# Two attention blocks with a gate on one core: score matmuls issued twice at accumulator closings, first loads on one queue, last output tiles summed in freed banks

## Chip, cores and metric

One core of one Trainium2 chip. The metric is device time in microseconds (us) of one execution; lower is better. The kernel before took 888.87 us at first (median of 3 runs, 887.62 to 891.12).

Engine names: PE is TensorE (matmul), PEld its weight loads, ACT is ScalarE, DVE is VectorE, POOL is GpSimd, SP is SyncE, which only issues transfers. "Granted clock" is the share of full speed that the throttle lets TensorE run at; the trace shows only 1.00 and 0.50.

## The reference, cut

```python
# x: (1, 2048, 512) bf16; 32 heads of 16
def _A_ref(x, wqkv, wo):                 # full attention
    q, k, v = split(x @ wqkv)
    p = softmax(einsum("bhqd,bhkd->bhqk", q, k) * 16 ** -0.5)
    return merge(einsum("bhqk,bhkd->bhqd", p, v)) @ wo

def _B_ref(x, wqkv, wo):                 # each query sees 8 keys, 2 apart
    ...
g = sigmoid((x * gate_w).sum(-1, keepdims=True))
return g * _A_ref(x, A_wqkv, A_wo) + (1 - g) * _B_ref(x, B_wqkv, B_wo)
```

Attention A costs 32 x 2048 x 2048 exponentials. ACT computes most of them, and DVE the rest with a polynomial.

## The kernel before

The program is written out by a planner (`Plan`) that simulates the engines with assumed durations and decides in which order each engine's instructions are emitted. Every change of an assumed duration can therefore reshuffle the order of all engines.

The main loop fills a PSUM ring of 3 or 2 banks with score matmuls, and ACT takes the exponential of the whole ring bank group in one instruction:

```python
def f():                                             # one fill of the ring, on PE
    for s_, (p_, t, j) in enumerate(units):
        qk_mm(ring[:, s_, :], p_, t, j)              # start=True: overwrites its bank
    ...                                              # (cut: one more unit for DVE)
yield ("pe", 0, dur, f)
...
def f():                                             # then, on ACT
    A.activation(out=st["pT"][:, 0:n, :], in_=ring[:, 0:n, :], func=ACT.Exp, ...)
```

The products with V are accumulated in one bank, `acc`, over a period (four heads, 512 queries); 32 periods follow each other. At the end of a period `acc` is closed: DVE copies it out, and until then PE can add nothing to it. So that PE looks busy to the clock's throttle, gaps are filled with dummy matmuls that add zero to the open `acc` or write an idle bank:

```python
HAM = 3.4133
share = 0.70
def idle_fill(self, st, room):
    ...
    have = sum(b - max(a, lo) for a, b in self.streamed)   # streaming in the last 3.41 us
    need = min(gap, self.share * self.HAM - have)
    ...                                                    # fill `need` with dummies
```

The loads of the first microseconds, and the times at which the planner assumes that they have landed:

```python
A.dma_start(out=wkr[:], in_=a_w3[:, :, D:2 * D])           # all of K's weights, ACT's queue
for sc in range(NC):                                       # four chunks of x, SP's queue
    SP.dma_start(out=xr[sc // 2][:, sc % 2], in_=...)
A.dma_start(out=wqr[:], in_=a_w3[:, :, 0:D])
...
XARR = (6.0, 8.0, 10.0, 12.0)
```

K's first projections are evicted by DVE (`kt_all`), which then takes their maximum (`kmax_all`). The last query chunk's output is computed in two pieces because one of its inputs comes very late: 7 of 8 products go to an SBUF tile `fpart`, and after the last period one product is added:

```python
def part():
    V.tensor_copy(out=fpart["t"][:, tt, :], in_=w.t[:])
...
yield ("pe", tt, MM + SW, tail, "w")                       # the eighth product
yield from out_steps(t, w, fpart["t"][:, tt, :], tt)       # DVE adds, SP stores
```

## Time and profile before

| kernel before | |
|---|---|
| span of the profiled run | 886.6 us |
| ACT busy | 839.2 us, 95% |
| first exponential starts | 20.84 us |
| stream of 726 exponentials, first start to last end | 854.31 us |
| last exponential's end to the end of the span | 11.50 us |
| mean granted clock | 0.978 |

From the page of the kernel before: the span; busy time with its share of the span and the number of instructions; the granted clock in 40 slices, in tenths; and two groups of instructions with "busy, mean ns | idle before, releaser".

```profile
span 886.6 us, 15806 instructions
...
PE 768.4 (87%) x5958; PEld 270.6 (31%) x6020; DVE 772.5 (87%) x1354; ACT 839.2 (95%) x751; POOL 619.2 (70%) x594
...
PEclk9799999999999999999999999999997999999999
...
L283 ACT ACTIVATE pT<-ring 128x1536 bf16<-128x1536 f32 x726 | 831.0, 1301 | 26.6 <-PE ring L283 16.8
L283 PE MATMUL ring<-qt,kt_all 32*128 32x512 bf16 x1814 | 288.2, 387 | 88.0 <-ACT pT L283 76.6
```

ACT is the engine that bounds the stream, and its idle time is mostly waiting for the ring to be filled (16.8 us). Where these waits lie is seen in stretches of 10 us (columns: stretch, its length, busy time of each engine with the count of instructions, granted clock, DMA share, GB/s); kernel before:

```profile
30.00:40.00 10.00, 9.78 (x74) 2.71 (x72) 5.72 (x12) 8.57 (x8) 0.00 (x0) 0.60 0.00 1
...
660.00:670.00 10.00, 7.92 (x53) 2.70 (x51) 8.66 (x17) 8.34 (x7) 9.69 (x11) 0.81 0.43 145
670.00:680.00 10.00, 9.55 (x56) 2.52 (x57) 7.02 (x12) 7.38 (x7) 9.84 (x9) 0.68 0.00 0
...
400.00:410.00 10.00, 9.02 (x67) 3.04 (x68) 8.29 (x17) 9.88 (x10) 5.10 (x8) 1.00 0.08 27
```

Where the clock is full, ACT is busy 9.88 of 10 us; where it is granted 0.60 to 0.81, only 7.4 to 8.6. In this profile the clock is low from 27.8 (for 10.24 us), 287.2 (3.41), 372.6 (6.83), 427.2 (3.41), 666.1 (10.24) and 799.2 us (3.41), and in a last stretch that the end of the kernel cuts. The complete ones are all multiples of 3.41 us, as the Trainium skill has it ("TensorE: Matmul & The Clock Gate", Part 1): two clock levels, decided in free-running windows of 3413 ns by how busy PE was.

The chain of waits of the kernel before in the first 24 us (start us, length us, what):

```profile
1.77 9.22 DMA xr<-in_A_x_dram
11.00 0.05 issue
11.04 1.08 PE xt L283 x16
...
15.97 0.69 DVE kmax_all L283
...
17.25 0.67 DVE kt_all L283
...
17.95 0.70 DVE kmax_all L283
...
20.84 3.71 ACT pT L283 x3
```

The chain to the first exponential begins with a load: x's third chunk lands at 11.0 us, and only then its 16 transposes (`xt`) start. Over the profile the four chunks' transposes start at 6.29, 8.94, 11.04 and 12.81 us.

The end of the kernel before, from its timeline (start us, length us, engine, line, operation, [idle before <- releaser]):

```profile
875.20 1.96 PE L283 MATMUL w<-ident,z 128*32 128x512 bf16 x9
875.61 0.69 DVE L283 COPY accS<-acc 128x512 f32<-128x512 f32 x1 [3.58 <-PE acc L283]
877.09 0.66 PE L283 MATMUL w<-identf,accS 128*128 128x128 f32 x4
...
880.10 1.29 DVE L283 TENSOR_TENSOR osb<-w,fpart 128x512 bf16<-128x512 f32 x2 [0.48 <-PE w L283]
...
882.62 1.30 DVE L283 TENSOR_TENSOR osb<-w,fpart 128x512 bf16<-128x512 f32 x2 [1.22 <-DMA out_dram<-osb]
```

Nine dummies delay the transposes of the last accumulator by 0.8 us, and the third output waits 1.22 us for a store to free its buffer.

### The profile page before, as it was taken

What the parts mean: (1) busy time and instruction counts of PE and PEld (TensorE: products, weight loads), DVE (VectorE), ACT (ScalarE), POOL (GpSimd) and SP (SyncE); (2) the same over time, 40 slices, a digit from 0 to 9 for tenths busy, and PEclk for the clock granted to TensorE, in tenths of its full rate; (3) what the DMA queues carried; (4) which work ended last, traced back from release to release, by engine and by line L of the source; (5) the groups of instructions that cost most, each with busy time, mean ns of one, the idle gap of its engine ahead of it and who ended that gap; (6) DMA issues with size and microseconds to landing.
All of it is one profiled execution on the core that took longest, in us unless ns stands there. A gap on an engine that the chain in (4) does not pass through costs nothing.

```text
span 886.6 us, 15806 instructions
## 1 busy us (share of the span) xinstructions
PE 768.4 (87%) x5958; PEld 270.6 (31%) x6020; DVE 772.5 (87%) x1354; ACT 839.2 (95%) x751; POOL 619.2 (70%) x594
## 2 busy tenths in 40 slices
PE   7998889998898888889889998888889988878886
PEld 4332333333223233222223233323322223222222
DVE  5689889988989899989888889999997989998885
ACT  3999999999999999989999999999998999999994
POOL 2000283899797899897898989898999798964000
PEclk9799999999999999999999999999997999999999
DMA  8002213330414230320030403113021230100000
GB/s 286 2 1 95 65 39 115 111 120 28 147 35 143 75 105 24 109 80 28 8 119 31 131 28 115 55 54 108 1 89 43 78 120 14 58 8 1 1 1 25
DMA packets 54653, 59.78 MB, mean 67 GB/s; under 512 B 2592, under 2 KB 51232, under 8 KB 54576
## 3 DMA queue, kind: packets, MB, share of 16 engines
q1 hardware_dynamic: 52992, 57.71, 20.4%
q10 hardware_dynamic: 1584, 1.05, 0.4%
q8 instruction: 47, 0.77, 0.4%
q14 instruction: 30, 0.25, 0.1%
HBM read 46.14 MB, written 12.62 MB: 66 GB/s over the span
## 4 chain that ended last, share of the span: by engine, by line
ACT 44%; PE 21%; issue 18%; DVE 15%; DMA 1%; POOL 0%; SPq 0%; another core or an unknown queue 0%; ACTq 0%; DVEq 0%
ACT pT L283 44%; PE w L283 9%; DVE ta L283 8%; PE ring L283 7%; PE acc L283 6%; DVE pd L283 2%; DMA xr<-in_A_x_dram 1%; DVE lg L283 1%; DVE accS L283 1%; DVE kt_all L283 0%; ACT lg L283 0%; DVE ssum L283 0%; DVE kvs L283 0%; DVE kmax_all L283 0%; DVE kpk L283 0%
## 5 line engine op out<-in xcount | busy, mean ns | idle before, releaser
L283 ACT ACTIVATE pT<-ring 128x1536 bf16<-128x1536 f32 x726 | 831.0, 1301 | 26.6 <-PE ring L283 16.8
L283 PE MATMUL ring<-qt,kt_all 32*128 32x512 bf16 x1814 | 288.2, 387 | 88.0 <-ACT pT L283 76.6
L283 DVE SCALAR_TENSOR_TENSOR ta<-ta,w 128x512 f32<-128x512 f32 x468 | 309.9, 681 | 5.1
L283 POOL TENSOR_TENSOR prod<-prod 128x512 f32<-128x512 f32 (+1 forms) x208 | 241.3, 1172 | 6.0
L283 PE MATMUL acc<-pT,vp_all 128*17 128x512 bf16 x1814 | 232.8, 391 | 0.1
L283 PEld LDWEIGHTS <-kt_all 32*128 32x128 bf16 x2048 | 105.0, 91 | 336.3 <-issue 320.4
L283 DVE TENSOR_SCALAR ta<-w 128x512 f32<-128x512 uint16 x234 | 158.4, 685 | 43.5 <-PE w L283 42.0
L283 PE MATMUL acc<-ident,z 128*32 128x512 bf16 (+4 forms) x756 | 170.3, 339 | 9.1 <-DVE accS L283 9.0
L283 DVE SCALAR_TENSOR_TENSOR pd<-ta,w 128x512 uint16<-128x512 f32 x234 | 157.1, 679 | 2.5
L283 POOL TENSOR_TENSOR prod<-ksh,qb 128x512 f32<-128x512 bf16 x128 | 145.7, 1166 | 11.4 <-DMA ksh<-kv_scr 9.2
L283 POOL TENSOR_TENSOR prod<-vsh,lg 128x512 f32<-128x512 bf16 x128 | 136.5, 1099 | 10.6 <-DVE lg L283 8.3
L283 PE MATMUL w<-qt,kt_all 32*128 32x512 bf16 x234 | 88.5, 388 | 1.3 <-DVE pd L283 1.2
L283 POOL TENSOR_SCALAR mq<-qpk 128x512 f32<-128x512 bf16 x12 | 7.5, 628 | 106.9 <-DVE qpk L283 106.9
L283 PE MATMUL acc<-pd,vp_all 128*17 128x512 bf16 x234 | 81.0, 391 | 0.0
L283 PEld LDWEIGHTS <-z 128*32 128x32 bf16 x796 | 54.2, 95 | 84.6 <-issue 65.6
L283 PEld LDWEIGHTS <-vp_all 128*17 128x17 bf16 x2048 | 43.9, 88 | 90.4 <-issue 88.8
L283 PE MATMUL w<-bw,xT 128*128 128x512 bf16 x160 | 49.1, 394 | 5.8 <-DVE pd L283 2.8
L283 PEld LDWEIGHTS <-xT 128*128 128x128 bf16 x512 | 31.8, 98 | 38.1 <-issue 26.1
L283 POOL TENSOR_TENSOR lg<-lg,mx 128x256 f32<-128x256 f32 x16 | 10.1, 631 | 44.6 <-DVE mx L283 44.6
L283 DVE CAST kvs<-w 128x512 bf16<-128x512 f32 x32 | 22.0, 687 | 12.1 <-PE w L283 11.9
L283 DVE COPY accS<-acc 128x512 f32<-128x512 f32 x32 | 21.8, 682 | 3.6 <-PE acc L283 3.6
L283 PE MATMUL w<-identf,accS 128*128 128x128 f32 x128 | 21.9, 296 | 0.1
(97 smaller groups left out, 439.2 us busy)
## 6 DMA issues: line engine op xcount, KB each, us to landing
ksh<-kv_scr SPq DMA_DIRECT2D x16, 1024.0 KB
vsh<-kv_scr SPq DMA_DIRECT2D x16, 1024.0 KB
kv_scr<-kvs SPq DMA_DIRECT2D x16, 256.0 KB
kt_all<-k_scr SPq DMA_DIRECT2D x6, 512.0 KB
q_scr<-qpk SPq DMA_DIRECT2D x24, 128.0 KB
qt<-q_scr SPq DMA_DIRECT2D x24, 128.0 KB
xr<-in_A_x_dram SPq DMA_DIRECT2D x4, 512.0 KB
out_dram<-osb SPq DMA_DIRECT2D x16, 128.0 KB
```

Source lines behind the costliest of these rows:

```text
L283: return chain_on(self._key, f(*a, **k))
```

## The change

Four intents:

1. *Closings.* While `acc` is closed and the planner's estimate of streaming in the last window is under 0.60, the ring's score matmuls are issued twice. They overwrite, so the result is the same and PE is busier. This adds 64 matmuls.
2. *Head, loads.* All first loads go to SP's queue in order of need, and of K's and Q's weights only the 128 columns needed first.
3. *Head, evictions.* The first head group's four K evictions move to ACT; DVE takes the maximum straight from PSUM.
4. *End.* When the ring is no longer needed, its banks become two tensors, both named `last`, of 3 and of 2 banks. The last chunk's tiles 2 and 3 sum all 8 products there, without the detour through SBUF (ACT copies them out and stores them); the last copy of `acc` is split between ACT and DVE.

```diff
-    A.dma_start(out=wkr[:], in_=a_w3[:, :, D:2 * D])
+    SP.dma_start(out=wkr[:, :, 0:128], in_=a_w3[:, :, D:D + 128])
     for sc in range(NC):
         SP.dma_start(out=xr[sc // 2][:, sc % 2], ...
-    A.dma_start(out=wqr[:], in_=a_w3[:, :, 0:D])
+    SP.dma_start(out=wqr[:, :, 0:128], in_=a_w3[:, :, 0:128])
     SP.dma_start(out=wv[:], in_=a_w3[:, :, 2 * D:3 * D])
+    SP.dma_start(out=wkr[:, :, 128:D], in_=a_w3[:, :, D + 128:2 * D])
+    SP.dma_start(out=wqr[:, :, 128:D], in_=a_w3[:, :, 128:D])
...
-    XARR = (6.0, 8.0, 10.0, 12.0)
+    XARR = (5.0, 6.9, 8.8, 10.7)
+    WARR = (3.4, 11.2)
+    TWICE = 0.60
...
+        if i == 0:                                      # K evictions
+            yield ("spawn", k_top(prio, lambda: top(w.t[:]), left, done))      # DVE: maximum
+            yield ("act", 0, 0.60, lambda: A.activation(out=kt, in_=w.t[:], func=ACT.Identity, ...))
...
             def f():
-                for s_, (p_, t, j) in enumerate(units):
-                    qk_mm(ring[:, s_, :], p_, t, j)
+                shut = acc_open[0]
+                twice = (shut is not None and not any(row_left[shut])
+                         and P.have(P.now + dur) < TWICE * P.HAM)
+                for _ in range(1 + twice):
+                    for s_, (p_, t, j) in enumerate(units):
+                        qk_mm(ring[:, s_, :], p_, t, j)
+                more = MM * twice                       # the planner is told: it may reorder
...
+    def end_banks(rname, n):
+        yield ("acq", rname, 9)
+        t = ps.tile([128, n, QW], FP32, tag=rname, bufs=1, name="last")
+        ...                                             # each bank of it goes to pool "e"
...
+    def direct_job(tt):                                 # tiles 2 and 3 of the last chunk
+        w = Bank("e")
+        ...                                             # 8 products into w
+        def ev():
+            A.copy(out=st["o"][:], in_=w.t[:])
+        yield ("act", 0, 0.60, ev)
+        yield ("act", 0, 0.06, lambda: A.dma_start(out=out2d[...], in_=st["o"][:]))
```

(Cut: the split copy of `acc`, `last` used for the last transposes too, one more rule for which units go to DVE in the last period, and a limit of the planner that is lifted once the ring is spent.)

## The prediction

> **What bounds it now.** The scalar engine (ACT): busy 839 us, 95% of the span (page, first part). Its stream of exponentials runs from 20.8 to 875.1 us (timeline) in 726 instructions; the compiled order of the changed kernel has the same 726, and as many units on VectorE (DVE). So the middle can only gain what ACT waits. I add up 16 us of ACT gaps over 0.15 us there, nearly all where the granted clock is 0.50: 27.8-38.1, 287.2-290.7, 372.6-379.4, 427.2-430.6, 666.1-676.4 and 799.2-802.7 us. By busy time in stretches of 10 us (windows view), ACT loses about 1.5 us in the first, and 1.8, 2.8, 1.3, 4.3 and 1.0 in the others. The low stretches last 3.41, 6.83 or 10.24 us. The Trainium skill ("TensorE: Matmul & The Clock Gate", Part 1) has a two-level clock set by activity in free-running windows of 3413 ns; this trace agrees. Adding up the time in which matmuls stream in such windows, each drop after 40 us follows one under about 0.45 (0.335, 0.336, 0.40, 0.43, 0.45); four of these five contain the closing of an accumulator.
>
> **Middle.** 64 extra score matmuls, about 29 doubled fills at 26 of 31 closings, 0.21 us of streaming each, 0.06 of a window. Sliding the window over the trace, I estimate 3.8 drops per run before and 2 after (those at 0.335 need more than one doubled fill). At 2.1 us a drop: -3.5 to -5 us. The extra 0.21 us hides behind an ACT instruction of 0.9 to 1.3 us.
>
> **Head.** First exponential at 20.84 us. PE waits for input only 0.58 and 0.39 us (at 8.9 and 11.0 us); before the first transposes it runs dummy matmuls until 6.3 us, as many as before, so an earlier first load buys nothing. The K evictions (0.75 us each) leave DVE, but in the compiled order ACT's eviction and DVE's maximum of one bank wait for each other, so the last pair stays serial; DVE's queueing goes, 0.3 us. First exponential -0.5 us.
>
> **Tail.** 11.1 us from the last accumulation (875.6) to the end. Gone: 0.8 us of dummy matmuls ahead of the transposes, and the third output's wait for a buffer (1.2 us). But the compiled order has new waits between engines on the tile `last`: the ACT half of the accumulator copy precedes the DVE half; denominators, normalizing and projection matmuls take turns; ACT's first output copy waits for DVE's second, the last matmul for that copy, and both ACT output DMAs follow both copies. Summing trace durations: about 11.5 us, +0.4. Some matmuls leave 840-860 us, where ACT lost 1 us: -0.5 us.
>
> **Sum.** -0.5 - 4.4 - 0.5 + 0.4: about 883.5 us, 80% range 879 to 888. Faster by over 2% 0.02, within 2% 0.97, slower 0.01.
>
> **What would show it.** About two low-clock stretches after 40 us instead of five; ACT gaps down from 16 to 11 us; first exponential at 20.0 to 20.6; tail 10.5 to 12; ACT busy up only by the K evictions and last copies (+4 us).
>
> **What would make it wrong.** The windows run freely, so drops differ from run to run; luck in one profile moves the time by 4 us. Doubled fills could delay ACT where PE is behind. The head could gain more if the loads set its pace. The tail's waits could cost less than I added.

## The result, and the profile after

878.0 us after (median of 4 runs, 876.26 to 881.81) against 888.25 before (median of 4): ratio 0.9884, 95% interval 0.9845 to 0.9924. Ratios here are the mean time of one kernel's fast runs over that of the other's of the same rounds, so not quite the ratio of the medians quoted. The change is inside 2%, as predicted, but 878.0 is 5.5 us under the predicted 883.5 and 1 us below the low end of its range. The profiled run is the slowest of the four (881.81 us); all runs here were in the fast state, or single runs of unknown state.

| | before | after |
|---|---|---|
| span of the profiled run | 886.6 | 880.0 |
| ACT busy | 839.2 | 842.6 |
| first exponential | 20.84 | 19.12 |
| stream of exponentials | 854.31 | 849.23 |
| last exponential's end to the end | 11.50 | 11.69 |
| mean granted clock, profiled run | 0.978 | 0.980 |
| mean granted clock, the four runs after | | 0.988 |

The page of the kernel after, same lines:

```profile
span 880.0 us, 15956 instructions
...
PE 771.3 (88%) x6062; PEld 268.1 (30%) x6062; DVE 767.9 (87%) x1346; ACT 842.6 (96%) x758; POOL 619.4 (70%) x594
...
PEclk9799999999999999999999999879999999999999
...
L288 ACT ACTIVATE pT<-ring 128x1536 bf16<-128x1536 f32 x726 | 830.1, 1290 | 19.9 <-PE ring L288 10.9
L288 PE MATMUL ring<-qt,kt_all 32*128 32x512 bf16 x1878 | 294.2, 387 | 87.0 <-ACT pT L288 77.0
```

ACT's wait for the ring fell from 16.8 to 10.9 us; the number of exponentials did not change. Stretches of 10 us of the kernel after:

```profile
30.00:40.00 10.00, 10.00 (x67) 2.70 (x66) 6.18 (x13) 8.54 (x9) 0.00 (x0) 0.68 0.00 1
...
580.00:590.00 10.00, 9.80 (x56) 2.48 (x52) 7.03 (x14) 7.96 (x8) 9.84 (x10) 0.54 0.00 1
660.00:670.00 10.00, 7.87 (x71) 2.88 (x65) 9.14 (x18) 9.76 (x10) 9.69 (x11) 1.00 0.38 118
770.00:780.00 10.00, 8.32 (x66) 2.95 (x64) 8.38 (x17) 9.46 (x10) 7.27 (x8) 0.85 0.02 8
```

The stretch 660 to 670, a closing that was low before, is at full clock (ACT 9.76 instead of 8.34). But the stretch at 580, where the clock was full before, is now low (ACT 7.96; before 8.66). Low stretches of this run: 26.1 (10.24 us), 285.5 (3.41), 562.0 (6.83), 579.1 (10.24), 777.0 (3.41): four after 40 us, leaving out one that the end of the kernel cuts, where I had predicted about two.

The chain of waits of the kernel after, first 24 us:

```profile
1.47 4.59 PE heat L288 x12
6.06 1.01 PE xt L288 x16
...
9.91 0.91 PE xt L288 x16
...
15.49 0.70 ACT kt_all L288
16.19 0.02 issue
16.21 0.70 DVE kmax_all L288
...
19.12 4.21 ACT pT L288 x4
```

The load is gone from the chain. The transposes of the four chunks start at 6.00, 7.44, 9.75 and 11.51 us. ACT's eviction and DVE's maximum of the last K bank do follow one another (15.49, then 16.21), as predicted. The Trainium skill says why an order is needed ("PSUM — Partial Sum Buffer", section "PSUM bank collisions raise a hardware error"): two engines must not access one bank and quadrant at once, two readers included.

The end of the kernel after, from its timeline:

```profile
869.28 0.37 ACT L288 COPY accS<-acc 128x256 f32<-128x256 f32 x1 [0.94 <-PE acc L288]
869.69 0.42 DVE L288 COPY accS<-acc 128x256 f32<-128x256 f32 x1 [1.53 <-ACT accS L288]
...
871.93 0.43 DVE L288 TENSOR_TENSOR otok<-last,rden 128x256 bf16<-128x256 f32 x1 [0.40 <-PE last L288]
872.41 0.59 PE L288 MATMUL last<-bwo,obt 128*128 128x512 bf16 x2 [0.52 <-DVE otok L288]
...
874.17 1.34 DVE L288 TENSOR_TENSOR osb<-last,fpart 128x512 bf16<-128x512 f32 x2 [0.48 <-PE last L288]
...
875.54 0.59 ACT L288 CAST osc<-last 128x512 bf16<-128x512 f32 x1 [5.89 <-DVE osb L288]
876.18 0.38 PE L288 MATMUL last<-awo,oT 128*128 128x512 bf16 x1 [1.40 <-ACT osc L288]
876.59 0.59 ACT L288 CAST osc<-last 128x512 bf16<-128x512 f32 x1 [0.46 <-DMA out_dram<-osb]
```

The predicted waits are all there: ACT's half of the copy before DVE's (both read the one bank `acc`); PE's output products and DVE's `rden` and `otok` in turns; ACT's first `osc` after DVE's second `osb`; the last matmul after that `osc` (1.40 us idle). Most of these waits are between instructions that touch *different banks* of one tensor. The program shows it: tiles 2 and 3 sum in banks 0 and 1 of the 3-bank `last`. Its bank 2 holds the transposed accumulator and then tile 1's eighth product. ACT's first `osc` reads bank 0 and waits for DVE's second `osb`, which reads bank 2; the last matmul writes bank 1 and waits for that `osc`.

### The profile page after: what moved, and what is told of

Read it like the earlier page. It is cut to its first block, busy times and chain, and to the rows that moved or that the text cites. A ratio compares the mean times of both kernels' runs of the same rounds, so it can differ in the third digit from the quotient of the medians.

```text
span 880.0 us, 15956 instructions
## 1 busy us (share of the span) xinstructions
PE 771.3 (88%) x6062; PEld 268.1 (30%) x6062; DVE 767.9 (87%) x1346; ACT 842.6 (96%) x758; POOL 619.4 (70%) x594
## 4 chain that ended last, share of the span: by engine, by line
ACT 48%; PE 22%; issue 19%; DVE 11%; DMA 0%; ACTq 0%
ACT pT L288 47%; PE w L288 8%; PE ring L288 7%; PE acc L288 6%; DVE ta L288 5%; DVE pd L288 1%; DVE lg L288 1%; PE heat L288 1%; PE last L288 0%; ACT lg L288 0%; DVE accS L288 0%; DVE ssum L288 0%; PE xt L288 0%; DVE kvs L288 0%; DVE kpk L288 0%
## 5 line engine op out<-in xcount | busy, mean ns | idle before, releaser
L288 ACT ACTIVATE pT<-ring 128x1536 bf16<-128x1536 f32 x726 | 830.1, 1290 | 19.9 <-PE ring L288 10.9
L288 PE MATMUL ring<-qt,kt_all 32*128 32x512 bf16 x1878 | 294.2, 387 | 87.0 <-ACT pT L288 77.0
L288 PE MATMUL acc<-ident,z 128*32 128x512 bf16 (+6 forms) x750 | 168.6, 340 | 5.9 <-DVE accS L288 5.4
L288 PEld LDWEIGHTS <-z 128*32 128x32 bf16 x774 | 51.9, 95 | 82.7 <-issue 65.5
L288 PE MATMUL w<-bw,xT 128*128 128x512 bf16 x192 | 51.2, 390 | 3.2 <-DVE pd L288 1.6
L288 DVE COPY accS<-acc 128x512 f32<-128x512 f32 (+1 forms) x32 | 21.5, 673 | 1.8 <-ACT accS L288 1.5
L288 POOL TENSOR_TENSOR obb<-ob,prod 128x512 bf16<-128x512 f32 x16 | 20.4, 1272 | 1.3
```

What stands on the lines that cost most here:

```text
L288: return chain_on(self._key, f(*a, **k))
```

## Experiments

My theory after seeing the result: the head gained about 1.7 us, not 0.5, because the loads had paced it; the sums at 840 to 860 us gained about 1.2; the end gained nothing because of waits between the banks of `last`; the rest, some 4 us, is less low clock thanks to the doubled fills. Rivals: the middle's gain is not the copies but another order of the planner, or luck with the free-running windows; the end would be no faster without those waits.

Eighteen runs were made: e1, e2 and e16 are the two kernels without an edit, and e15 repeats e8. All gave correct results. "5 rounds" are 6 runs of the kernel, with runs of the kernel before on the same chip.

### How far luck goes

**e1_before_again** and **e2_after_again**, later **e16_after_third**: the two kernels without an edit, 5 rounds.

> The kernel before, unchanged, to get the granted clock of each of its runs. Theory (clock drops): its runs differ because the number of 3.41 us low windows differs; time falls with the clock along one line, about 0.8 us for each 0.002 of mean clock, and its mean clock is 0.976 to 0.985. Rival (the drops are not what moves the time): times do not follow the clock. Ratio to before 1.000.

> The changed kernel, unchanged. Theory: mean clock 0.985 to 0.994 in most runs, 876 to 882 us, again along a line of time against clock, and that line lies about 2.5 us under the line of the kernel before (head and tail), the rest of the 10 us being clock. Rival (the gain is mostly head and tail): the lines lie 6 us or more apart.

> The changed kernel again: 878.5 to 880.5 us at clock 0.983 to 0.988; last accumulation to the end 10.8 us.

Measured: e1 887.65 us (ratio 1.0005, interval 0.9977 to 1.0033); e2 879.4 (0.9915, 0.9884 to 0.9946); e16 880.5 (0.9912, 0.9885 to 0.9939). First exponential at 21.09, 19.45 and 19.30 us.

What follows: pooled over all runs, the kernel before has a mean of 887.0 us at a granted clock of 0.9762 (61 runs), the kernel after 879.5 at 0.9857 (16 runs): 7.4 us. Single runs scatter by 2.1 to 2.4 us (standard deviation), and the clock explains most of it: over all kernels, time within one kernel falls 4.4 us per 0.01 of mean clock (correlation -0.92, and 1.0 us is left over). From this scatter, a mean of six runs is uncertain by about 1 us, and the difference of two such means by about 1.4 us (one standard error). I use this slope below to compare kernels "at equal clock" (0.985): 883.1 before, 879.8 after. The four runs had 0.988; with the pooled clock they would have read about 1 us more.

### The head

**e5_before_loads**: only the loads (and the planner's arrival times `XARR`, `WARR`) in the kernel before, one look. **e6_before_kevac**: only the K evictions on ACT, one look. **e10_before_head**: both, 5 rounds.

```diff
 # e5, to before
-    A.dma_start(out=wkr[:], ...)          # and wqr
+    SP.dma_start(out=wkr[:, :, 0:128], ...)   # ... as in the change
-    XARR = (6.0, 8.0, 10.0, 12.0)
+    XARR = (5.0, 6.9, 8.8, 10.7)
 # e6, to before
+        if i == 0:                        # as in the change: ACT evicts, DVE takes the maximum
```

> The kernel before with the reordered first loads alone. The prediction's reading (dummy matmuls hold the first transposes, loads set no pace): first exponential at 20.5 to 21.1 us, as before (20.84, 21.09, 20.98 in three profiles). Theory now (the second and third chunk of the input set the pace, and the eviction chain only follows): transposes of chunks 1 to 3 start near 7.8, 10.2 and 12.0 us instead of 9.0, 11.1 and 12.9, and the first exponential comes 0.9 to 1.2 us earlier, at 19.7 to 20.0.

> The kernel before with the K evictions moved to the scalar engine alone, loads as before. Theory: 0.3 to 0.6 us earlier first exponential, at 20.3 to 20.6, since the last pair stays serial (eviction, then maximum) and only VectorE's queueing goes. Rival (evictions carry the head's gain): 1.2 us or more earlier, under 19.7.

> The kernel before with both head changes (loads and K evictions) and nothing else. First exponential at 19.1 to 19.5 us, 1.5 us under before. Theory A: clock 0.974 to 0.978 and 885.2 to 886 us. Theory B (any reshuffled order has its own number of drops): clock outside 0.973 to 0.978 by 0.003 or more, with the time following at 0.38 us for each 0.001.

Measured: first exponential at 19.57 us (e5), 20.48 (e6) and 19.69 (e10), against 20.97 in the mean of three profiles of the old head (20.84, 21.09, and 20.98 in e4 below) and 19.29 in three of the kernel after. Times 882.82, 882.38 (single runs), 881.93 (ratio 0.9955, 0.9914 to 0.9996). The transposes of e5, from its timeline:

```profile
6.03 1.07 PE L283 MATMUL xt<-ident,xr 128*128 128x128 bf16 x16 [0.27 <-DMA xr<-in_A_x_dram]
...
7.51 1.07 PE L283 MATMUL xt<-ident,xr 128*128 128x128 bf16 x16
...
9.79 1.06 PE L283 MATMUL xt<-ident,xr 128*128 128x128 bf16 x16
...
11.54 1.06 PE L283 MATMUL xt<-ident,xr 128*128 128x128 bf16 x16
```

What follows: the loads alone bring 1.4 us, the evictions alone 0.5, and in the order of the kernel before the two together no more than the loads. The first chunk moved by only 0.26 us (6.29 to 6.03), chunks two to four by 1.3 to 1.4: the later loads set the pace. That K's weights, on another queue at the same time, had slowed x is the likely reason; no run separates it from the smaller amount that is loaded first. From 4 to 14 us the DMA engines move 320 to 368 GB/s in both profiles, so what changed is what is loaded in front of x, and not a faster rate. e10 met none of its expectations: the first exponential came 0.2 us after the expected range, the time is under theory A's, and the clock (0.9793) lies between theory A's and theory B's. At equal clock e10 is 3.2 us under the kernel before, which is more than its head; the rest is an effect of the new order in the middle, which I did not trace to one place.

### The doubled fills

**e3_after_once**: the kernel after in its finished order, with the 64 second copies not emitted. **e4_before_twice**: the order of the kernel before with 55 copies put in, of which the planner is not told. 5 rounds each.

```diff
 # e3, to after
-                for _ in range(1 + twice):
+                for _ in range(1):
 # e4, to before: the lines of the change, without "more"
+                for _ in range(1 + twice):
```

> The changed kernel in its own order, with only the 64 second copies of score matmuls left out. Theory: the closings lose their extra activity, clock falls back to 0.976 to 0.985 and the time rises 4 to 7 us over the changed kernel, to 882 to 885. Rival (schedule, head and tail made the gain): within 1.5 us of the changed kernel.

> The kernel before in its own order, with 55 second copies of score matmuls added at the closings and nothing else. Theory: 4 to 7 us faster than before, 881 to 884, clock 0.985 to 0.993, first exponential unchanged at 20.8 us. Rival: within 1.5 us of before, or slower if the copies hold up the scalar engine.

Measured: e3 881.45 us (0.9937, 0.9908 to 0.9966), mean 881.70 at clock 0.9823, against e2 of the same chip, mean 879.84 at 0.9847. e4 884.18 (0.9962, 0.9938 to 0.9986), mean 883.91 at 0.9815, against e1, 887.73 at 0.9752.

What follows: in the old order the copies are worth 3.8 us (3.0 against all runs of the kernel before), less than the 4 to 7 I had expected. In the finished order the means differ by 1.9 us, which is not clear of noise (the intervals of e2 and e3 overlap); neither the expected 4 to 7 us nor the rival's 1.5 or less is what was measured. Most of both differences goes with the clock: at equal clock e3 and e2 differ by 0.8 us, e4 and e1 by 1.0. But in the finished order, without any copy, the clock is already at 0.9823. So part of what I had given to the copies is not theirs.

**e9_after_plain**: `TWICE` set to zero, so that the planner makes an order that knows no copies. **e13_plain_copies**: the order of e9 with 57 copies put in unplanned.

```diff
 # e9, to after
-    TWICE = 0.60
+    TWICE = 0.0
 # e13, to after
-                more = MM * twice
+                more = 0.0
```

> The changed kernel without doubled fills, planned without them (head, tail and loads as changed). Theory A (the copies are what raises the clock; orders do not matter): mean clock as in the kernel before, 0.974 to 0.978, about 884.5 us. Theory B (the changed kernel's other shifts in order also spare drops, as the run that left the copies out of the finished order suggests, clock 0.982): 881 to 882.5 us, clock 0.981 to 0.984.

> The order of the version without doubled fills (e9: 879.8 us at clock 0.979), with 57 second copies put in at the closings and nothing moved. Theory (copies raise the clock at no cost; planning them in cost the tail 1.9 us): clock 0.984 to 0.988, tail from the last accumulation 8.8 us, 876.5 to 878 us, at least 1.5 us under e9 and under the changed kernel. Rival (the copies themselves cost what the clock gives): 879 to 880.5 us at clock 0.985.

Measured: e9 879.37 us (0.9926, 0.9892 to 0.996), mean 879.83 at clock 0.979; the end, from the last accumulation on, took 8.83 us instead of 10.79. e13 879.11 (0.9906, 0.988 to 0.9933), mean 879.41 at 0.9798, end 8.82 us.

What follows: e9 is as fast as the kernel after, without any doubled fill. It loses clock (0.979 against 0.9857) and gains 2 us at the end, because in its order the waits between banks do not arise (see e7 below). It also has one exponential fewer on ACT (725; so has e13), and takes 0.5 us less from exponential 676 to the end of the last. Neither theory of e9 had foreseen this: it is faster than both said, at a clock between theirs. My expectation of e13, that the copies raise its clock, failed: the two means differ by 0.4 us. The comparison is loose, since the two ran in different calls on chips 1 and 6: measured against the kernel before of its own call (means 886.3 and 887.7), e13 gains 1.8 us more than e9. So a small worth of the copies is not excluded there. That it depends on the order that they are put into would fit 3.0, 1.9 and 0.4 us, but is not shown by them.

**e12_after_share80**: more dummies in ordinary gaps (`share` 0.70 to 0.80), 5 rounds.

> The changed kernel with its dummy fills planned for 80% of a window instead of 70%. Theory (windows under the threshold are left because the plan overrates its own activity): clock 0.989 or more, 1 to 2 us faster than the changed kernel. Rival (dummy matmuls get in the way of fills): at equal clock 1 us or more slower, no gain in time.

Measured: 879.0 us (0.9926, 0.9892 to 0.996), mean 879.56 at clock 0.985. The same as after: more dummies of this kind buy nothing that these runs can show, and the expected clock of 0.989 did not come.

### The end

**e7_before_tail**: only the change of the last chunk in the kernel before, one look.

```diff
 # e7, to after: old loads, old K evictions, and
-    TWICE = 0.60
+    TWICE = 0.0
```

> The kernel before with the change of the last chunk alone (no doubled fills, first loads and K evictions as before). Theory: from the last accumulation to the end 10.8 us instead of 11.07, and over the last 66 exponentials (from number 660 on) 1.1 us less than before at full clock, because half of the last chunk's sums leave the stretch 840 to 855 us. First exponential 20.8 to 21.1. Rival (the freed banks shorten the end itself): 2 us or more less from the last accumulation to the end.

Measured: 884.59 us, single run at clock 0.976; end 8.81 us instead of 11.07. My theory, that this part of the change brings little at the end, failed here, and the rival's expectation of 2 us or more came true. e7 and e9 have the same statements for the end as the kernel after; only the planned order differs, and with it which tile got which bank. Both programs sum tiles 2 and 3 in the two banks of the 2-bank `last`, and everything that DVE reads lies in the 3-bank one, so that ACT's `osc` need not wait for DVE. The timeline of e9 agrees; DVE's two `osb` run from 875.76 to 877.05:

```profile
876.19 1.07 ACT L288 CAST osc<-last 128x512 bf16<-128x512 f32 x2 [4.17 <-PE last L288]
```

**e8_after_tail_free** and **e15_tail_free_again** (no further edit): the kernel after, with tiles 2 and 3 of the last chunk in ordinary work banks that are tensors of their own, SP storing them, and `acc` copied out by DVE alone. 5 rounds each.

```diff
 # e8, to after
-        w = Bank("e")
+        yield ("wait", ev_spent)
+        w = Bank()
...                                             # (cut: the event, and the undivided copy of acc)
-        yield ("act", 0, 0.06, lambda: A.dma_start(out=out2d[...], in_=st["o"][:]))
+        yield ("sp", 0, 0.1, lambda: SP.dma_start(out=out2d[...], in_=st["o"][:]))
```

> The changed kernel with the last two output tiles summed in the two work banks (tensors of their own) instead of banks of the tensor 'last', their outputs issued by the SyncE queue, and the accumulator copied by VectorE alone. Theory (the tail keeps its 10.8 us because accesses to different banks of one tensor are made to wait for each other): no engine waits for another bank any more, and the last accumulation to the end takes 8.0 to 8.6 us; 2.2 to 2.8 us under the changed kernel at equal clock. Rival (the output DMAs or the chain copy, transpose, normalize, transpose sets it): 10.3 us or more.

> The version with the tail freed of waits between banks, again. 877.3 to 878 us at clock 0.985 to 0.987, 1.5 to 2 us under the changed kernel of the same rounds; last accumulation to the end 8.9 us.

Measured: end 8.90 us in both. Times 879.14 (0.9908, 0.9875 to 0.9941) and 877.47 (0.9899, 0.9865 to 0.9933). The end of e8, from its timeline:

```profile
869.38 1.29 DVE L288 TENSOR_TENSOR osb<-last,fpart 128x512 bf16<-128x512 f32 x2 [0.48 <-PE last L288]
...
869.81 1.07 ACT L288 CAST osc<-w 128x512 bf16<-128x512 f32 x2 [4.89 <-PE w L288]
...
871.13 0.87 SPq L288 DMA_DIRECT2D out_dram<-osc  x2
```

DVE's two `osb` and ACT's two `osc` now overlap: ACT starts 0.43 us after DVE, waits for PE and not for DVE, and does both without a gap. In the kernel after it started 1.37 us later than DVE (874.17 to 875.54), and its second copy came 1.05 us after the first. At equal clock e8 and e15 are at 878.0, against 879.8 after: the 1.9 us of the end (10.79 to 8.90) arrive in the time. The rival, that the end would be no faster without those waits, is out; the end is still 0.3 us longer than the 8.0 to 8.6 that I had expected. e8 changes three things at once: the banks, the queue of the last stores, and the copy of `acc`. But e9 leaves the last two as in the kernel after, its divided copy still takes turns (ACT at 871.65, DVE at 872.05), and its end takes 8.83 us. So it is the banks.

### The start

The early low stretch (10.24 us in the profile of both kernels) is the longest common loss, so I tried to remove it with copies before 34 us.

**e11_after_start**: copies also before 34 us, planned. **e14_after_start_same**: the same in the finished order of the kernel after, unplanned. **e17_before_start**: only such copies (30), in the order of the kernel before. 5 rounds each.

```diff
 # e11, to after
-                         and P.have(P.now + dur) < TWICE * P.HAM)
+                         and P.have(P.now + dur) < TWICE * P.HAM) or P.now < 34.0
 # e14, to after
-                for _ in range(1 + twice):
+                for _ in range(1 + (twice or P.now < 34.0)):
 # e17, to before
+                for _ in range(1 + (P.now < 34.0)):
```

> The changed kernel with score fills doubled also in the first 34 us, 35 more matmuls. Every profile so far has 6.8 to 20.5 us of half clock beginning between 20 and 29 us. Theory (activity there is too low, small matmuls of 64 columns and of one column): that stretch shrinks to at most 6.8 us, mean clock up by 0.003 to 0.008, 1 to 2.5 us faster than the changed kernel at 879.4. Rival (the copies delay the scalar engine in a stretch where the tensor engine is the slower one): slower by 0.5 us or more.

> The changed kernel in its own order, with second copies also of the fills planned before 34 us, nothing moved. Theory (e11 was slow because its whole order was reshuffled): within 1 us of the changed kernel at equal clock, and the low stretch that begins at 20 to 29 us shorter than 10.2 us, or gone. Rival (the copies hold up the scalar engine in the first 40 us): first 44 exponentials 2 us or more longer than in the changed kernel.

> The kernel before in its own order with second copies of the fills planned before 34 us (30 matmuls), nothing else. If the early stretch costs before more than the changed kernel (mean 15 us of low clock against 9 us), its clock rises by 0.007 to 0.010, to 0.983 to 0.986, and it is 3 to 4 us faster, 883 to 884. In the changed kernel the same copies gave 0.0067 and 2.4 us. If the head does not matter here, 0.004 to 0.007 and about 2.4 us.

Measured: e11 885.99 us (1.0007, 0.9971 to 1.0043), so the expectation failed: the early stretch was short, but the planner, told of the longer fills, had made an order that is 5.6 us slower at equal clock (885.4 against 879.8); ACT waited 17.8 us for the ring, against 8.8 in e2. e14 876.9 (0.9881, 0.9856 to 0.9906), mean 877.15 at clock 0.9923 (e16, the kernel after: 879.91), with no low stretch before 559 us in its profile. e17 886.48 (0.9994, 0.9955 to 1.0033), in two groups: three runs at 882 to 884 us with clocks of 0.986 to 0.991, three at 889 to 895 with 0.970 to 0.974. The profile, the only one, fell into the second group:

```profile
20.00:30.00 10.00, 9.62 (x87) 3.38 (x84) 3.64 (x6) 4.97 (x5) 0.00 (x0) 0.54 0.06 18
30.00:40.00 10.00, 10.00 (x94) 2.42 (x91) 3.76 (x6) 7.40 (x6) 0.00 (x0) 0.50 0.00 0
```

What follows: PE is nearly always busy and the clock is still low; it stayed so for 23.9 us. Every fill is doubled at half speed, ACT is busy 4.97 and 7.40 of 10 us, and from the first exponential to the 22nd this run takes 32.9 us, 6.8 more than the kernel before. Two other profiles tell the copies' part from that of the early fall: in e4 and e7 the clock also falls early (at 20.3 and 20.6 us, for 20.5 us), no fill is doubled yet, and the same stretch takes 28.7 and 28.8 us. So the early fall alone takes about 2.7 us more than the kernel before, and the copies some 4 on top. Where the clock happens to fall at 20.9 us, these copies cost what they should save. My expectation of a plain gain failed in half of the runs. The new head is not shown to be immune: e14 and e18 together had 12 runs without such a case (judged by their clocks, 0.985 or more), which is no proof.

**e18_best**: e8 and e14 together, 5 rounds, the version that the experiments pointed to.

> The changed kernel with the freed tail (e8, e15) and second copies also of the fills planned before 34 us, not counted in the plan (e14). Clock 0.990 to 0.993, last accumulation to the end 8.9 us, 875 to 876 us, 3.5 to 4.5 us under the changed kernel and 11 to 12 us under before.

Measured: 875.05 us (872.79 to 879.96), against 885.68 before on that chip: 0.9882, interval 0.9849 to 0.9915; mean 875.69 at clock 0.9918; end 8.90 us. That is 3.8 us under the pooled mean of the kernel after, which was not run in the same rounds; the ratio to the kernel before overlaps with that of e14. At equal clock it is 878.7, 1.1 us under the kernel after.

## Why the prediction was right or wrong

What each term was to be, and what it is. Pooled times differ by 7.4 us, where the prediction's terms add up to 5.0. The base that they imply, 888.5, was 1.5 us above the pooled 887.0, and the four runs lie 1.0 us (mean) under the pooled 879.5. These two, a base from few runs and luck with the clock, are 2.5 of the 5 us by which the mean, 878.5, misses 883.5; without that luck the result would have been at the low end of the predicted range, 879 to 888. The rest of the miss is in the terms.

| term | predicted | measured | from |
|---|---|---|---|
| first exponential | -0.5 | -1.7 | 20.97 to 19.29, means of three profiles each |
| low clock in the stream | -4.4 | -4.2 | estimated: 0.0095 of clock times 4.4 us per 0.01 |
| waits at 840 to 860 us | -0.5 | -1.2 | see below |
| last exponential to end | +0.4 | +0.2 | 11.50 to 11.69 |
| sum | -5.0 | -6.9 | 7.4 measured; 0.5 not placed |

1. *The head: wrong, and this is the step that failed.* The prediction put it as "so an earlier first load buys nothing". I had looked at PE's waits (0.58 and 0.39 us) and at the dummies before the first chunk. That holds for the *first* chunk, which moved by 0.26 us. But the changed loads also bring the later chunks sooner, and the chain of waits of the kernel before began with the load of the third one, 9.22 us long. e5 shows 1.4 us from the loads alone, where the prediction counted zero; the evictions alone, 0.5 us in e6, were near its 0.3. Even its own two waits, 0.97 us together, should have warned me. I had listed this among what could make the prediction wrong, yet gave it no size.

2. *The sums: right mechanism, term too small.* From exponential 676 (counted from 0) to the last, start to start, all profiles with the old end take 57.06 to 57.09 us. The profiles of the kernel after (including e2, e16, e8, e15, e14, e18) take 55.87 to 55.88, e3 in the same order 56.01. In stretches of 10 us, first before, then after:

```profile
840.00:850.00 10.00, 9.83 (x64) 2.85 (x64) 7.37 (x12) 9.27 (x9) 0.00 (x0) 1.00 0.00 0
850.00:860.00 10.00, 8.47 (x72) 2.91 (x71) 7.56 (x15) 9.57 (x10) 0.00 (x0) 1.00 0.01 2
...
840.00:850.00 10.00, 7.97 (x72) 2.92 (x66) 9.67 (x17) 10.00 (x10) 0.00 (x0) 1.00 0.01 2
850.00:860.00 10.00, 8.12 (x68) 2.85 (x65) 9.25 (x18) 10.00 (x10) 0.00 (x0) 1.00 0.00 0
```

ACT (the fourth busy time) does not wait there any more. From exponential 676 on, its waits fell from 1.15 to 0.28 us, one of them left, at 834.8 us; I had counted half of 1 us. In e7, which has the change of the end alone, they fell to 0.28 as well. The other 0.3 us lie in the exponentials' own durations, and I did not look for the cause.

3. *The end: right.* The new waits were read from the compiled order and cost what the change saved, within 0.2 us. What I had not seen is that they are an accident of which tile got which bank: the same statements take 8.8 us in e7 and e9.

4. *The middle: size right, cause half right.* The mean clock moved about as predicted, and ACT's gaps over 0.15 us fell by 4.4 us, about as predicted (from 17.8 to 13.5 by the sum over the traces; the prediction had 16 to 11). But the prediction's "nearly all where the granted clock is 0.50" was too much: it is 11.7 of the 17.8. And "About two low-clock stretches after 40 us" was wrong: there were four in the first profile, three in e2, six in e16. Fewer of them lie at closings (none of the four in the first profile, two of three in e2, three of six in e16; four of five before), and those that do are mostly milder: the one of 10.24 us at 660 to 673 us in the kernel before, e1, e5, e10 and e17 cost ACT 4.3 us each time, and a drop at a closing at most 2.4 in profiles with doubled fills. But at most 2.1 in e3 too, in the finished order without any, so this need not be the copies' doing. The copies themselves are worth some 1.9 us in this order (e3, not clear of noise), not 4.4. My threshold of 0.45 of a window was not sharp: drops followed windows that I estimate at 0.43 to 0.51 busy in the kernel after, and none followed one at 0.441 in the kernel before and one at 0.436 in e2.

5. *What stays open.* Why the finished order has a higher clock (0.9823, e3) than the kernel before (0.9762) without any copy. The head is a candidate: the early low stretch lasted 10.2 to 20.5 us with the old head and 6.8 to 10.2 with the new one. But e17 shows that such stretches come out in two ways with the same program, and e10 with the new head had only 0.9793. Also open: order effects of 1 to 2 us in the middle at equal clock, and whether e18's copies at the start can meet the bad case of e17.

## What to carry to other kernels

Before saying that an earlier load buys nothing, follow the chain of waits to every chunk that the first result needs, not to the first chunk alone. Where a planner or scheduler decides the order, separate a change's effect from the reshuffling: build it once in the frozen order and once planned, since here the planned form lost 2 us at the end and made another change 5.6 us slower. Where a clock gate moves time between runs, record each run's granted clock and compare at equal clock, with enough runs, before giving a few microseconds to a cause.

## What the Trainium skill lacked or had wrong

- "TensorE: Matmul & The Clock Gate", section "HAM oscillation": it tells of waits long enough to cross a window that throttle the clock again. Here the clock also fell after windows in which I estimate PE streaming 0.34 to 0.51 of the time, and windows at 0.436 (e2) and 0.441 (the kernel before) had no drop. The page gives no busy share that keeps the clock up; these runs show that there is no sharp one in such an estimate.
- The same page does not say that more PE work at half clock can delay the work that matters: in e17 the clock stayed low for 23.9 us with PE busy 9.62 and 10.00 of 10 us, ACT was busy 4.97 and 7.40, and the first 22 exponentials took some 4 us longer than in e4 and e7, whose clock fell as early without the copies.
- The same page, Part 1, says the windows are free-running; it gives no size for a whole kernel's scatter. Here 61 runs of one program scatter by 2.4 us of 887, and time follows the mean granted clock by 4.4 us per 0.01.
- "PSUM — Partial Sum Buffer", section "PSUM bank collisions raise a hardware error": it asks for an order between engines on one bank and quadrant. In this program the banks of one multi-bank tensor were ordered against each other as well, which cost about 1.9 us (end 10.8 against 8.9 us in e8 and e15); the page does not warn that guarding by tensor is coarser than guarding by bank.
